# Attention on pooled keys and two feed-forward layers on one Trainium2 core: four changes of place, VectorE for GpSimd, GpSimd for TensorE

## The chip, the cores and the metric

The kernel runs on one core of one Trainium2 chip. The metric is the device time of one execution in microseconds. A time is the median of several runs; besides, one execution was taken apart by the hardware profiler, and every row below comes from that one. Engines are called as in the profile: PE is TensorE (PEld its weight load, which overlaps with PE), DVE is VectorE, ACT is ScalarE, POOL is GpSimd, and SP is the engine whose queue issues the DMAs.

## The reference

```
B, H, S, D = 8, 8, 576, 64
k_p = k.reshape(B, H, 72, 8, D).mean(axis=3)          # keys and values: means of 8 rows
v_p = v.reshape(B, H, 72, 8, D).mean(axis=3)
attn = softmax(q @ k_p.T / 8)                          # 576 x 72 per head
x = (attn @ v_p) -> [4608 tokens, 512]
h = x @ w_in1;  g = 0 if h <= -1, h if h >= 1, else (h + 1)**2 / 4;  x2 = g @ w_out1
h = x2 @ w_in2; r = max(h, 0);  out = (r * r) @ w_out2    # w_in 512 x 2048, w_out 2048 x 512
```

All is float32. The two layers take nearly all of the work.

## The kernel before

**Split products.** A float32 product is made of three products in the type fp32r: each operand is split in a high part (a copy that ScalarE rounds to fp32r) and a low part (the difference, by VectorE), and TensorE adds high times high, high times low and low times high. For the weights the parts are `wihi`, `wilo`, `wohi`, `wolo`; for the activations `xhi`, `xlo`, `gh`, `gl`.

**Steps.** Layer one goes in 9 blocks of 512 tokens by 16 pieces of the hidden dimension, in 144 steps, and 16 more steps start layer two. In step s, `gemm1(s)` makes `ph` in 12 matmuls (L666), ScalarE and VectorE make `g` from it (L689, L690, L699) and split it (L701, L707), and `gemm2(s - 2)` adds to four PSUM banks in 12 matmuls (L738). `ph` has two buffers: `gemm1(s + 2)` waits for VectorE's `g` of step s. In the steps for which `whole` says so, `gemm2` takes `g` and the weight unsplit, in plain float32 (L727); each such matmul shows as two records in the trace.

**Attention inside the steps.** The queries come in 36 tiles of 128 tokens. A tile's attention is cut in units, and tables (`slots`, `pool_at`) put at most two into a step: scores (`pss`, L372), softmax on VectorE and ScalarE, the product with the values (`px`, L488). The attention of the first four tiles stands ahead of step 0, in the head of the program. The rest of layer one's blocks wait for the tiles that make their input, so all goes in one order.

**Pooling.** Keys and values of a batch come in 8 pieces (4 of keys, 4 of values, two heads each) into a pool of three buffers. For batch 0, VectorE adds rows for the keys and GpSimd for the values (L284), and TensorE does the rest. For batches below `ON_PE` TensorE does all the pooling, in matmuls of the raw piece with the identity (`pk`, L309, and `pv`, L329). For the others GpSimd pools each piece in three additions (L297 twice, L298), and TensorE only turns the pooled keys (L314).

**Queries.** Tiles below `TURNED` come by one or two DMAs and are turned by TensorE (`pq`, L356), which ScalarE copies out of PSUM. The others come by 16 or 32 small DMAs, already cut in blocks of 32, and VectorE turns each block (L347).

**Weights.** Every weight is mapped from the bits of its load by ScalarE, VectorE (L153, L156, L159) and one integer addition of GpSimd (L162): those of layer one in the head and steps 0 to 15, those of layer two (`z`) in 16 groups between steps 28 and 140. A group (`prepare_w2`) takes two pieces, keeps their quarters as high and low parts in DRAM (`keep_w2`, tile `cb`, L172 and L173), makes four sums of quarters (L196 to L199, for a product with 7 instead of 8 partial products) and keeps these too. The second layer then reads them back.

**Order.** Instructions are put on each engine's queue by a scheduler that works from the program's order; each engine then takes its own queue in order, and the one SP queue issues all DMAs.

Of the kernel before, what the change touches and what calls it, by code (L numbers as in the profile page):

```python
# [23 lines left out]

TURNED = 11

# [5 lines left out]
def pooled_attention_moe_moe(  # L32
# [59 lines left out]

    ON_PE = 3
    NK = -(-SP // TR)
# [73 lines left out]

    def keep_w2(kind, g, n, two, lo_on):

        c = cv.tile([P, 2, 2, HB], F32R, tag="st", name="cb")
        nc.scalar.activation(out=c[:, :, 0, :], in_=two, func=AF.Copy)  # L172
        lo_on.tensor_tensor(out=c[:, :, 1, :], in0=two, in1=c[:, :, 0, :].bitcast(F32), op=ALU.subtract)  # L173
        nc.sync.dma_start(out=w2c[kind][g][:, n:n + 2], in_=c.bitcast(F32))

    def prepare_w2(kind, g):

        two = []
        for i in range(2):
            f = g + i * NG  # L180
            stage_w(kind, 1, f)
            yield
            conv = convert_w(kind, 1, f)
            for _ in conv:
                pass
            two.append(halves(w_sb.pop((kind, 1, f))).rearrange("p (a c) -> p a c", a=2))
            yield
            keep_w2(kind, g, 2 * i, two[i], nc.vector)
            yield
# [5 lines left out]
        s1, s2, s3, s4 = s12[:, 0, :], s12[:, 1, :], s34[:, 0, :], s34[:, 1, :]  # L195
        nc.gpsimd.tensor_tensor(out=s1, in0=a21, in1=a22, op=ALU.add)  # L196
        nc.gpsimd.tensor_tensor(out=s2, in0=s1, in1=a11, op=ALU.subtract)
        nc.gpsimd.tensor_tensor(out=s3, in0=a11, in1=a21, op=ALU.subtract)
        nc.gpsimd.tensor_tensor(out=s4, in0=a12, in1=s2, op=ALU.subtract)  # L199
        yield  # L200
        keep_w2(kind, g, 4, s12, nc.gpsimd)
        yield
        keep_w2(kind, g, 6, s34, nc.gpsimd)
        yield
# [74 lines left out]
    def pool_kv(nm, b, p):  # L279
        if b == 0:  # L280

            a = kv_t[nm, b, p]
            for w in (4 * D, 2 * D):
                (nc.vector if nm == "k" else nc.gpsimd).tensor_tensor(  # L284
                    out=a[:, :, 0:w], in0=a[:, :, 0:w], in1=a[:, :, w:2 * w], op=ALU.add
                )
        if b < ON_PE:
# [227 lines left out]
    for t in range(TB0, NTILE):  # L515
# [10 lines left out]
        if t in first_tile:  # L526
            b = first_tile.index(t)
            todo.update({2 * c - 2 + i // 2: ("k", b, i) for i in (0, 2)})
            if b < ON_PE:
                todo.update({at_v: ("v", b, i) for at_v, i in zip(((7, 9), (37, 39))[b - 1], (0, 2))})  # L530
            for i in range(2 * NP if b >= ON_PE else 0):
# [94 lines left out]
    def whole(kind, s):  # L626

        return kind == "o" and s < KF

# [524 lines left out]
```

## Time and profile before

| | |
|---|---|
| median of 3 runs | 1673.24 us (1672.28, 1673.24, 1678.28) |
| the profiled execution's own time | 1679.75 us |
| its span | 1677.7 us |
| mean granted clock of TensorE | 0.989 of full speed |
| busy: PE, DVE, ACT, POOL | 98%, 74%, 53%, 20% of the span |

The span runs from the first to the last instruction; the execution's time holds 2.05 us more. The clock of 1.00 is 2.4 GHz, and 0.50 is 1.2 GHz; shares between them are means over a stretch. The busy shares are means over stages: the head (0 to 43 us), steps 0 to 15 with the weights of layer one (43 to 215 us), layer one with the preparation of layer two's weights (up to 884 us, where GpSimd's last instruction ends), then the rest of layer one and layer two.

### The profile page before, as it was taken

What the parts mean: (1) busy time and instruction counts of PE and PEld (TensorE: products, weight loads), DVE (VectorE), ACT (ScalarE), POOL (GpSimd) and SP (SyncE); (2) the same over time, 40 slices, a digit from 0 to 9 for tenths busy, and PEclk for the clock granted to TensorE, in tenths of its full rate; (3) what the DMA queues carried; (4) which work ended last, traced back from release to release, by engine and by line L of the source; (5) the groups of instructions that cost most, each with busy time, mean ns of one, the idle gap of its engine ahead of it and who ended that gap; (6) DMA issues with size and microseconds to landing.
All of it is one profiled execution on the core that took longest, in us unless ns stands there. A gap on an engine that the chain in (4) does not pass through costs nothing.

```text
span 1677.7 us, 23589 instructions
## 1 busy us (share of the span) xinstructions
PE 1640.4 (98%) x7952; PEld 1322.4 (79%) x7952; DVE 1237.9 (74%) x1973; ACT 885.0 (53%) x1603; POOL 327.6 (20%) x299
## 2 busy tenths in 40 slices
PE   7899999999999899999999999999999999999998
PEld 6665788888887687878888888888888878887886
DVE  5998578888888888888886452569557856885585
ACT  5655455656566465766666542346435533553353
POOL 3444144542435515231230000000000000000000
PEclk7999999999999999999999999999999999999999
DMA  9475535435354445443543085567686777677675
GB/s 240 134 217 152 144 83 155 148 108 161 112 158 141 118 122 181 123 132 103 192 170 128 7 295 176 170 193 231 191 255 218 207 204 238 213 207 227 194 206 135
DMA packets 276728, 284.72 MB, mean 170 GB/s; under 512 B 151168, under 2 KB 179840, under 8 KB 276608
## 3 DMA queue, kind: packets, MB, share of 16 engines
q1 hardware_dynamic: 276608, 283.21, 56.4%
q8 instruction: 64, 1.05, 0.3%
q14 instruction: 56, 0.46, 0.1%
HBM read 218.10 MB, written 65.01 MB: 169 GB/s over the span
## 4 chain that ended last, share of the span: by engine, by line
PE 84%; DVE 8%; DMA 3%; issue 2%; ACT 1%; POOL 1%; SPq 1%; DVEq 0%; POOLq 0%; ACTq 0%
PE ph L666 22%; PE acc L738 20%; PE dp L1012 10%; PE cp L1003 10%; PE dq L1012 5%; PE cr L1003 5%; PE cq L1003 3%; PE dr L1012 3%; PE px L488 2%; PE pss L372 2%; PE acc L727 2%; DVE wilo L221 1%; DMA w<-w2i 1%; DVE wolo L221 1%; DMA st<-in_moe_w_out_dram 1%
## 5 line engine op out<-in xcount | busy, mean ns | idle before, releaser
L666 PE MATMUL ph<-xhi,wihi 128*128 128x512 f32 x576 | 233.4, 406 | 6.8 <-DVE g L699 5.7
L666 PE MATMUL ph<-xlo,wihi 128*128 128x512 f32 x576 | 226.4, 393 | 0.0
L666 PE MATMUL ph<-xhi,wilo 128*128 128x512 f32 x576 | 226.2, 393 | 0.0
L960 ACT ACTIVATE gh<-g 128x512 fp32r<-128x512 f32 x224 | 139.7, 630 | 151.7 <-DVE g L1029 48.0
L738 PE MATMUL acc<-gh,wohi 128*128 128x512 f32 x512 | 205.9, 402 | 0.0
L738 PE MATMUL acc<-gh,wolo 128*128 128x512 f32 x512 | 200.1, 391 | 1.5 <-DVE wolo L221 1.5
L738 PE MATMUL acc<-gl,wohi 128*128 128x512 f32 x512 | 200.2, 391 | 0.0
L1003 PE MATMUL cp<-x,w 128*128 128x512 f32 x768 | 187.0, 390 | 1.0 <-DMA w<-w2i 0.7
L768 DVE TENSOR_TENSOR gl<-g,gh 128x512 fp32r<-128x512 f32 x224 | 151.3, 687 | 47.6 <-ACT gh L960 46.2
L1003 PEld LDWEIGHTS cp<-x,w 128*128 128x128 f32 x768 | 143.5, 188 | 33.6 <-issue 2.2
L221 DVE TENSOR_TENSOR wilo<-wi,wihi 128x512 fp32r<-128x512 f32 x144 | 123.4, 857 | 58.3 <-ACT wihi L217 57.3
L1012 PE MATMUL dp<-gh,w 128*128 128x512 f32 x512 | 161.5, 389 | 0.0
L707 DVE TENSOR_TENSOR gl<-g,gh 128x512 fp32r<-128x512 f32 x144 | 114.3, 794 | 56.7 <-ACT gh L701 54.1
L666 PEld LDWEIGHTS ph<-xhi,wihi 128*128 128x128 f32 x576 | 109.2, 190 | 35.2 <-DVE g L699 6.1
L217 ACT ACTIVATE wihi<-wi 128x512 fp32r<-128x512 f32 x144 | 89.8, 624 | 81.2 <-PE ph L666 81.0
L666 PEld LDWEIGHTS ph<-xhi,wilo 128*128 128x128 f32 x576 | 109.3, 190 | 23.5
L666 PEld LDWEIGHTS ph<-xlo,wihi 128*128 128x128 f32 x576 | 109.3, 190 | 22.4 <-issue 1.0
L701 ACT ACTIVATE gh<-g 128x512 fp32r<-128x512 f32 x128 | 80.3, 628 | 84.1 <-DVE g L699 83.5
L297 POOL TENSOR_TENSOR kv<-kv 72x512 f32<-72x512 f32 x80 | 93.7, 1173 | 158.4 <-DMA kv<-in_k_dram 81.6
L221 DVE TENSOR_TENSOR wolo<-wo,wohi 128x512 fp32r<-128x512 f32 x128 | 109.2, 853 | 15.3 <-ACT wohi L217 15.1
L1025 ACT ACTIVATE s<-cp 128x512 f32<-128x512 f32 x96 | 57.2, 595 | 118.7 <-PE cp L1003 118.7
L738 PEld LDWEIGHTS acc<-gh,wolo 128*128 128x128 f32 x512 | 96.3, 188 | 21.4 <-DVE wolo L221 2.9
(144 smaller groups left out, 3208.7 us busy)
## 6 DMA issues: line engine op xcount, KB each, us to landing
w<-w2i SPq DMA_DIRECT2D x224, 256.0 KB
w<-w2o SPq DMA_DIRECT2D x224, 256.0 KB
w2i<-cb SPq DMA_DIRECT2D x32, 512.0 KB
w2o<-cb SPq DMA_DIRECT2D x32, 512.0 KB
st<-in_moe_w_out_dram SPq DMA_DIRECT2D x31, 512.0 KB
st<-in_moe_w_in_dram SPq DMA_DIRECT2D x29, 512.0 KB
pd<-pad SPq DMA_DIRECT2D x32, 384.0 KB
z<-pd SPq DMA_DIRECT2D x96, 128.0 KB
```

The source lines that it names most:

```text
L217: nc.scalar.activation(out=hi, in_=src, func=AF.Copy)
L221: eng.tensor_tensor(out=lo, in0=src, in1=hi.bitcast(F32), op=ALU.subtract)
L297: nc.gpsimd.tensor_tensor(out=a[:, :, 0:w], in0=a[:, :, 0:w], in1=a[:, :, w:2 * w], op=ALU.add)
L666: nc.tensor.matmul(out=ph, lhsT=a[:, kk % a.shape[1], :], rhs=c[:, kk, :], start=(i == 0), stop=(i == 3 * KD - 1))
L701: act(out=gh, in_=g, func=AF.Copy)
L707: nc.vector.tensor_tensor(out=gl, in0=g, in1=gh.bitcast(F32), op=ALU.subtract)
L738: nc.tensor.matmul(out=o, lhsT=lhsT, rhs=rhs, start=(f == 0 and x == 0), stop=(f == KF - 1 and x == 2),)
L768: tt(out=out, in0=a, in1=b, op=ALU.subtract)
L960: act(out=hi, in_=a, func=AF.Copy)
L1003: nc.tensor.matmul(out=out[0], lhsT=w[:, a, k, :], rhs=xq[b, i][c][:, k, :], start=(n == 0 and i in (1, 2, 7)), stop=(n == 5), skip_group_ ...
L1012: nc.tensor.matmul(out=out[d], lhsT=w[:, a, d, :], rhs=x[c], start=(g == 0 and n == 0 and i in (1, 2, 7, 4)), stop=(g == NG - 1 and n == 2 ...
L1025: act(out=snaps[key], in_=a, func=AF.Copy)
```

## The change

Four things change. (1) The low parts and the sums in `prepare_w2` that GpSimd made are made by VectorE. (2) `ON_PE` goes from 3 to 2, so batch 2 is pooled by GpSimd, at places that `pool_at` gives, instead of by TensorE in matmuls; VectorE also adds the rows of batch 0's values. (3) `WHOLE` is 10: steps 0 to 9 instead of 0 to 15 take `gemm2` in unsplit float32, and steps 10 to 15 are split. (4) `TURNED` goes from 11 to 8.

```diff
+WHOLE = 10
-TURNED = 11
+TURNED = 8
...
-    ON_PE = 3
+    ON_PE = 2
...
-    def keep_w2(kind, g, n, two, lo_on):
+    def keep_w2(kind, g, n, two):
...
-        lo_on.tensor_tensor(out=c[:, :, 1, :], in0=two, in1=c[:, :, 0, :].bitcast(F32), op=ALU.subtract)
+        nc.vector.tensor_tensor(out=c[:, :, 1, :], in0=two, in1=c[:, :, 0, :].bitcast(F32), op=ALU.subtract)
...
-        nc.gpsimd.tensor_tensor(out=s1, in0=a21, in1=a22, op=ALU.add)
-        nc.gpsimd.tensor_tensor(out=s2, in0=s1, in1=a11, op=ALU.subtract)
-        nc.gpsimd.tensor_tensor(out=s3, in0=a11, in1=a21, op=ALU.subtract)
-        nc.gpsimd.tensor_tensor(out=s4, in0=a12, in1=s2, op=ALU.subtract)
+        nc.vector.tensor_tensor(out=s1, in0=a21, in1=a22, op=ALU.add)
+        nc.vector.tensor_tensor(out=s2, in0=s1, in1=a11, op=ALU.subtract)
+        nc.vector.tensor_tensor(out=s3, in0=a11, in1=a21, op=ALU.subtract)
+        nc.vector.tensor_tensor(out=s4, in0=a12, in1=s2, op=ALU.subtract)
         yield
-        keep_w2(kind, g, 4, s12, nc.gpsimd)
+        keep_w2(kind, g, 4, s12)
         yield
-        keep_w2(kind, g, 6, s34, nc.gpsimd)
+        keep_w2(kind, g, 6, s34)
...
             for w in (4 * D, 2 * D):
-                (nc.vector if nm == "k" else nc.gpsimd).tensor_tensor(
-                    out=a[:, :, 0:w], in0=a[:, :, 0:w], in1=a[:, :, w:2 * w], op=ALU.add
-                )
+                nc.vector.tensor_tensor(out=a[:, :, 0:w], in0=a[:, :, 0:w], in1=a[:, :, w:2 * w], op=ALU.add)
...
-                todo.update({at_v: ("v", b, i) for at_v, i in zip(((7, 9), (37, 39))[b - 1], (0, 2))})
+                todo.update({at_v: ("v", b, i) for at_v, i in zip((7, 9), (0, 2))})
...
-        return kind == "o" and s < KF
+        return kind == "o" and s < WHOLE
```

Lines up to 283 stand two further down in the changed kernel (L162 is L164 there, L221 is L223); from L297 on they are the same.

TensorE's queue at the place where batch 2's keys are pooled (step 15), before. `acc` are the banks of `gemm2`, `wo` a weight, `gw` an unsplit activation:

```order
L666 MATMUL ph<-xhi,wilo 128x512
L309 MATMUL pk<-ident,kv 64x72 x32
L727 MATMUL acc_685<-gw,wo_1345 128x512
L727 MATMUL acc_686<-gw,wo_1345 128x512
L727 MATMUL acc_687<-gw,wo_1345 128x512
L727 MATMUL acc_688<-gw,wo_1345 128x512
L309 MATMUL pk<-ident,kv 64x72 x32
L666 MATMUL ph<-xhi,wihi 128x512
```

The same place in the changed kernel:

```order
L738 MATMUL acc_688<-gh,wolo 128x512
L488 MATMUL px<-aT,vp 64x128 x8
L314 MATMUL pk<-ident,kp 128x72 x2
L738 MATMUL acc_688<-gl,wohi 128x512
L738 MATMUL acc_685<-gh,wohi 128x512
L738 MATMUL acc_685<-gh,wolo 128x512
L666 MATMUL ph<-xhi,wihi 128x512
L314 MATMUL pk<-ident,kp 128x72 x2
```

The 64 matmuls of the raw keys are gone for 4 turns of pooled keys, and the step's `gemm2` is split.

GpSimd's queue in the changed kernel around steps 8 to 12, where it stands between the additions that finish the weights of layer one (`wo`, `wi`, L164):

```order
L164 TENSOR_TENSOR wi_1146<-low_1148,wi_1146 128x512
L164 TENSOR_TENSOR wo_1238<-low_1240,wo_1238 128x512
L164 TENSOR_TENSOR wi_1242<-low_1244,wi_1242 128x512
L297 TENSOR_TENSOR kv<-kv 72x2x256
L297 TENSOR_TENSOR kv<-kv 72x2x128
L298 TENSOR_TENSOR kp<-kv 72x128
L164 TENSOR_TENSOR wo_1312<-low_1314,wo_1312 128x512
L297 TENSOR_TENSOR kv<-kv 72x2x256
L297 TENSOR_TENSOR kv<-kv 72x2x128
L298 TENSOR_TENSOR kp<-kv 72x128
```

Before, the same additions stand there with nothing between them:

```order
L162 TENSOR_TENSOR wi_1140<-low_1142,wi_1140 128x512
L162 TENSOR_TENSOR wo_1211<-low_1213,wo_1211 128x512
L162 TENSOR_TENSOR wi_1215<-low_1217,wi_1215 128x512
L162 TENSOR_TENSOR wo_1275<-low_1277,wo_1275 128x512
L162 TENSOR_TENSOR wi_1279<-low_1281,wi_1279 128x512
```

Two of batch 2's four pieces of keys are seen here; the first stands eight additions of weights further up, the fourth two further down.

VectorE's queue in the changed kernel at the first group of layer two's weights (`s` holds two sums of quarters, `cb` the parts that are kept):

```order
L707 TENSOR_TENSOR gl<-g,gh 128x512
L198 TENSOR_TENSOR s_2770<-z 128x256
L175 TENSOR_TENSOR cb<-z,cb 128x2x256
L199 TENSOR_TENSOR s_2770<-s_2770,z 128x256
L223 TENSOR_TENSOR wilo<-wi_402,wihi 128x512
L200 TENSOR_TENSOR z<-z 128x256
L201 TENSOR_TENSOR z<-z,s_2770 128x256
L699 SCALAR_TENSOR_TENSOR g<-ph,u 128x512
L175 TENSOR_TENSOR cb<-s_2770,cb 128x2x256
L175 TENSOR_TENSOR cb<-z,cb 128x2x256
L707 TENSOR_TENSOR gl<-g,gh 128x512
```

Before, the sums and the last two low parts of this group stand on GpSimd's queue:

```order
L196 TENSOR_TENSOR s_2712<-z 128x256
L197 TENSOR_TENSOR s_2712<-s_2712,z 128x256
L198 TENSOR_TENSOR z<-z 128x256
L199 TENSOR_TENSOR z<-z,s_2712 128x256
L173 TENSOR_TENSOR cb<-s_2712,cb 128x2x256
L173 TENSOR_TENSOR cb<-z,cb 128x2x256
```

Now `wilo`, `g` and `gl` of the steps stand behind these six on VectorE.

## Rows read from the trace of the kernel before

**Rows 1.** The page: span, and busy time of each engine.

```profile
span 1677.7 us, 23589 instructions
PE 1640.4 (98%) x7952; PEld 1322.4 (79%) x7952; DVE 1237.9 (74%) x1973; ACT 885.0 (53%) x1603; POOL 327.6 (20%) x299
```

**Rows 2.** Windows of 20 us: PE, PEld, DVE, ACT, POOL busy, PEclk, DMA share, GB/s.

```profile
60.00:80.00 20.00, 16.23 (x108) 10.90 (x107) 19.35 (x35) 15.11 (x30) 8.43 (x6) 1.00 0.79 225
...
120.00:140.00 20.00, 16.64 (x77) 10.48 (x77) 19.93 (x37) 12.44 (x23) 7.62 (x6) 1.00 0.56 156
...
160.00:180.00 20.00, 20.00 (x197) 13.76 (x196) 8.67 (x13) 7.67 (x16) 7.82 (x7) 1.00 0.48 131
```

**Rows 3.** Waits of PE: us in total, times, longest.

```profile
PE pk L309 <- DVE kv L284: 7.4, 3, 5.7
PE ph L666 <- DVE g L699: 5.7, 1, 5.7
...
PE pss L372 <- DVE xlo L501: 2.3, 2, 1.7
```

**Rows 4.** Timeline of PE: start, length, instructions; a whole, then a split `gemm2`.

```profile
161.21 3.60 PE L727 MATMUL acc<-gw,wo 128*128 128x512 f32 x8
164.74 1.09 PE L488 MATMUL px<-aT,vp 72*64 72x128 f32 x16
...
203.55 0.39 PE L738 MATMUL acc<-gh,wohi 128*128 128x512 f32 x1
...
206.27 3.66 PE L329 MATMUL pv<-kv,ident 72*72 72x128 f32 x32
```

**Rows 5.** Groups of PE's instructions by form, 160 to 215 us.

```profile
L329 PE MATMUL pv<-kv,ident 72*72 72x128 f32 x64 | 7.3, 272 | 0.0
...
L309 PE MATMUL pk<-ident,kv 72*64 72x72 f32 x128 | 4.4, 228 | 0.0
...
L356 PE MATMUL pq<-ident,q 128*128 128x128 f32 x8 | 1.2, 272 | 0.0
```

**Rows 6.** The chain that ended last, 500 to 600 us: start, length.

```profile
501.04 2.82 PE ph L666 x12
...
581.67 5.49 PE ph L666 x12
```

**Rows 7.** Timeline of DVE inside the longest wait of PE.

```profile
576.52 2.42 DVE L221 TENSOR_TENSOR wilo<-wi,wihi 128x512 fp32r<-128x512 f32 x1
```

**Rows 8.** Timeline of POOL, ahead of and inside that wait.

```profile
560.59 2.55 POOL L297 TENSOR_TENSOR kv<-kv 72x512 f32<-72x512 f32 x2 [13.63 <-DMA kv<-in_v_dram]
...
572.54 4.64 POOL L297 TENSOR_TENSOR kv<-kv 72x512 f32<-72x512 f32 x4
```

**Rows 9.** Groups of POOL's instructions by form, 240 to 860 us.

```profile
L297 POOL TENSOR_TENSOR kv<-kv 72x512 f32<-72x512 f32 x33 | 47.5, 1439 | 141.5 <-DMA kv<-in_v_dram 73.7 <-DMA kv<-in_k_dram 67.8
...
L297 POOL TENSOR_TENSOR kv<-kv 72x256 f32<-72x256 f32 x33 | 29.7, 901 | 2.5
L173 POOL TENSOR_TENSOR cb<-s,cb 128x512 fp32r<-128x512 f32 x14 | 20.8, 1488 | 0.0
...
L196 POOL TENSOR_TENSOR s<-z 128x256 f32<-128x256 f32 x14 | 11.9, 852 | 1.0
...
L298 POOL TENSOR_TENSOR kp<-kv 72x128 f32<-72x128 f32 x16 | 10.1, 642 | 2.2 <-PE pk L314 1.7
```

**Rows 10.** Groups of DVE's instructions by form, 240 to 860 us.

```profile
L221 DVE TENSOR_TENSOR wilo<-wi,wihi 128x512 fp32r<-128x512 f32 x99 | 88.5, 894 | 17.7 <-ACT wihi L217 17.5
...
L173 DVE TENSOR_TENSOR cb<-z,cb 128x512 fp32r<-128x512 f32 x27 | 19.2, 711 | 13.0 <-ACT cb L172 12.9
```

**Rows 11.** Line L221 from 885 us on, where POOL is idle: ns min/median/max.

```profile
L221 DVE TENSOR_TENSOR wolo<-wo,wohi x17: 681/684/693, 884.6 to 965.0; 128x512 fp32r<-128x512 f32 x17
```

**Rows 12.** Line L284, batch 0's sums on VectorE: ns min/median/max.

```profile
L284 DVE TENSOR_TENSOR kv<-kv x8: 420/554/689, 4.4 to 10.9; 72x512 f32<-72x512 f32 x4, 72x256 f32<-72x256 f32 x4
```

**Rows 13.** Timeline of SP's queue: part of the DMAs of one turned tile.

```profile
171.34 5.85 SPq L253 DMA_DIRECT2D q<-in_q_dram  x11
```

More of the change, by code (lines that the diff above doesn't have):

```diff
@@ L187, in prepare_w2 @@
             yield
-            keep_w2(kind, g, 2 * i, two[i], nc.vector)
+            keep_w2(kind, g, 2 * i, two[i])
             yield
```

## Prediction

> **What bounds the kernel now.** The page comes first: TensorE is busy for 1640.4 of 1677.7 us, VectorE for 1237.9 [rows 1]. So only some 37 us of the span can come from waits; anything more has to come from work that TensorE no longer does. The windows then show that the share hides two different stages [rows 2]. From 60 to 140 us VectorE is full (19.35 and 19.93 of 20 us) and TensorE is not: in the two windows shown it lacks 3.8 and 3.4 us. At 160 to 180 us it is the other way round, TensorE 20.00 and VectorE 8.67. From there to the end TensorE waits almost for nothing. The list of waits says where the rest is [rows 3]: 7.4 us in the head for VectorE's sums of the first keys, which nothing here touches; short ones such as 2.3 us for `xlo`, in the full stage; and one single wait of 5.7 us for `g`.
>
> That single wait, at 576 to 582 us, is worth a look, since it is made by what the change moves. GpSimd had stood still for 13.63 us for a piece of values and then worked without a break, 4.64 us of it in four additions of pooling [rows 8], with the sums of the weight quarters among them. VectorE's `wilo` took 2.42 us in it [rows 7], where one with GpSimd idle takes 0.684 [rows 11]. `g` stood behind it on VectorE's queue. After the wait the granted clock was down, and the first 12 matmuls took 5.49 us instead of 2.82 [rows 6]. So this event cost 5.7 + 2.7 = 8.4 us.
>
> **The change on TensorE.** All of this lies at 145 to 215 us, where TensorE is the bound.
> - A whole `gemm2` takes 164.74 - 161.21 = 3.53 us, a split one 206.27 - 203.55 = 2.72 us [rows 4]. Six steps change from the one to the other: -4.9 us. The price is paid elsewhere: a rounding of `g` and of `wo` on ScalarE, and `gl` and `wolo` on VectorE, 2 x 0.68 us a step [rows 11]. VectorE had over 11 us free in 20 there [rows 2], so I take nothing for it; if it came late by its whole length in all six steps it would be 8 us.
> - Batch 2's keys and values took 4.4 and 7.3 us [rows 5]; the four turns of pooled keys that come instead cost what four `pq` cost, half of 1.2 us [rows 5]: -11.1 us.
> - The `pq` of three tiles go, 0.6 us each: -1.8 us.
>
> That is -17.8 us. Busy times hold the tail of each run's last matmul, which the next one overlaps, so I take **-17** (15 to 18).
>
> **The change on GpSimd and VectorE, weights.** In 240 to 860 us GpSimd's low parts take 1.49 us each and a sum 0.85 [rows 9]. With two and four in each of 16 groups, 16 x (2 x 1.49 + 4 x 0.85) = 102 us of GpSimd's work go. On VectorE a low part takes 0.71 [rows 10], and a sum, of half the width, about the 0.42 us that is the least of batch 0's sums [rows 12]: 16 x (2 x 0.71 + 4 x 0.42) = 50 us more for VectorE. Part comes back at once: `wilo` takes 0.894 us on average in that stage [rows 10] against 0.684 undisturbed [rows 11], and if all subtractions with both inputs in SBUF (some 300: `wilo`, `wolo` and `gl`) lose 0.2 us each, that is 60 us of stretching for all that GpSimd does there; with some two fifths of its work gone, about 25 us. So VectorE gets some 25 us more work net over 620 us, 4 points. TensorE needs `g` only two steps later, so this costs nothing while VectorE's queue stays less than a step late. What hides it is that reserve, and if it is used up the price is an event like the one above, 8.4 us. That one itself I take as gone, since GpSimd's sums and low parts that lay between the poolings are: **-8.4 us**. Both ends: 0, if another takes its place, and -8.4.
>
> How hard the two engines hinder each other is also in the Trainium skill, "SBUF — State Buffer", section "Who interferes with whom": an instruction of VectorE with two inputs in SBUF and one of GpSimd that reads SBUF exclude each other, and the later one waits for the other's whole length. The 2.42 us of `wilo` agree with that [rows 7]; the average of 0.894 says that most instructions do not meet one. By the rule the gain could be up to the 102 us of VectorE's time; the time of the kernel would not change by it, because VectorE is not the bound in that stage.
>
> **The change in the full stage.** Here it costs. GpSimd's pooling of batch 2's keys now lies in steps 8 to 12, about 100 to 150 us: four pieces of 1.44 + 0.90 + 0.64 us [rows 9], 12 us. If it hinders VectorE as GpSimd does at 240 to 860 us (0.2 us on each 0.68 at a third of the time busy, and half of VectorE's instructions of a kind that is hindered), 12 us of it cost VectorE 4 to 6 us; the ends are 0 and 12. VectorE's queue has no reserve there, but it has one from 150 us on, so a part shows on TensorE: **+3 us**. The new DMAs of tile 8 come in here too: eleven DMAs of a turned tile keep SP's queue for 5.85 us [rows 13], so 16 hold back the weights' loads queued behind by some 7 us once; it is in the +3, because the loads run ahead of their use. Tiles 9 and 10 load later, where the queue and VectorE have room; VectorE's turn in place of ScalarE's copy is nothing there.
>
> **The head.** VectorE makes batch 0's eight sums of values, 8 x 0.554 = 4.4 us [rows 12], between 19 and 30 us, and is no longer hindered by GpSimd's. It holds free time there and the chain waits for TensorE most of the time: **+1 us** (0 to 4).
>
> **Sum.** Against the profiled execution's own 1679.75 us: -17 - 8.4 + 3 + 1 = -21.4, **1658 us**. The median is 6.5 us below that execution. If it lacks the single wait, the change is -13 from 1673.24 (1660); if it has it, -21.4 (1652). Both lie around the 1658 that I keep. A change of half a per cent, 8.4 us, is about what a measurement of this kernel tells from none; faster by that means below 1664.9.
>
> **Rivals.**
> - *The wait comes back elsewhere.* VectorE gets more work in the weights' stage, and GpSimd still stands behind late pieces and then catches up. For it: VectorE's waits for rounded weights are there already (17.5 us for `wilo`, 12.9 for `cb`) [rows 10]. Against it: in 620 us there was one such event. It gives 1658 + 8.4 = 1666 with one. Chance 0.16.
> - *GpSimd blocks VectorE for the whole length in the full stage*, 12 us instead of 3, and TensorE shows it all, since it already waits there. For it: 19.93 us of 20 busy [rows 2]. Against it: the average of 0.894. It gives 1658 + 9 = 1667. Chance 0.1. The rule of the Trainium skill that is named above, in "SBUF — State Buffer", would do just this if every addition met an instruction of VectorE.
> - *Slower: VectorE becomes the bound of the weights' stage.* Its first sum of a group needs the second piece's `z` from GpSimd, which stands behind pooling that waits up to 13.63 us for a piece [rows 8]. Before, GpSimd itself stood there; now VectorE stands, with `wilo`, `g` and `gl` of the steps behind it. A wait of VectorE longer than its reserve of about a step is an event of 8.4 us or more. From two on the gain is gone (1658 + 2 x 8.4 = 1675); three give 1683, slower than 1673.24 by 0.6%. Against it: ScalarE's copy of the same `z` waits for it already today, ahead of the step's `u`, and with 16 groups only one event shows. Chance 0.08.
>
> **Chances and range.** The forecast holds with 0.66. Faster: it, and a small part of the two mild rivals: 0.70. Same: most of these two: 0.22. Slower: 0.08. The range: below, the gains at their upper ends with no cost (1658 - 4 - 1, and the 1652 of the median) and some of TensorE's short waits in the full stage gone too, 1648; above, the two mild rivals and a little more, 1671. The likeliest case's own range is 1651 to 1664.
>
> **What would show it.** Right: in the new profile TensorE's busy time is down by about 17 us, with 128 records of L309 and 64 of L329 fewer and step 16 some 13 us earlier than before; no wait of 5 us between 240 and 860 us; VectorE's `wilo` near 0.8 us there; VectorE still full from 60 to 150 us, with TensorE's idle time there some 3 us above the old. Wrong: waits of PE for VectorE of several us in the weights' stage (third rival), idle time of PE at 100 to 150 us up by 10 (second), or the six split steps late by `wolo` or `gl`. A head that ends more than 4 us later would also break it, above all if the clock of TensorE rose later.

## The result, and the profile after

The changed kernel takes 1657.03 us (median of 4 runs, 1655.25 to 1657.76), the kernel before 1672.76 in the same series; the ratio is 0.9901, with a 95% interval of 0.9874 to 0.9928. It is faster by 1.0%, and 1 us off the forecast. The stages and the experiments show that the forecast is right as a total only, and by luck: terms of the sum were wrong by 12 us in one direction and by 13 in the other.

The page of the changed kernel; it answers to [rows 1]:

```profile
span 1654.9 us, 23309 instructions
...
PE 1616.5 (98%) x7776; PEld 1312.1 (79%) x7776; DVE 1269.4 (77%) x2092; ACT 889.0 (54%) x1610; POOL 245.5 (15%) x219
```

TensorE's busy time is down by 23.9 us and the span by 22.8, so TensorE is idle as long as before. The windows of the full stage and of the one behind it answer to [rows 2]:

```profile
60.00:80.00 20.00, 20.00 (x123) 14.04 (x122) 19.73 (x33) 12.48 (x25) 9.39 (x7) 0.93 0.83 247
...
120.00:140.00 20.00, 20.00 (x90) 13.90 (x90) 19.93 (x37) 13.63 (x26) 10.87 (x10) 1.00 0.70 185
...
160.00:180.00 20.00, 19.82 (x115) 16.04 (x115) 15.38 (x25) 12.90 (x25) 8.48 (x9) 1.00 0.32 99
```

VectorE (third pair) is as full as before, and GpSimd (fifth) does more, but TensorE no longer lacks 3.8 and 3.4 us in the first two. The waits of TensorE over the whole span answer to [rows 3]:

```profile
PE pk L309 <- DVE kv L286: 8.7, 3, 6.3
PE ph L666 <- DVE g L699: 5.8, 4, 2.2
PE pss L372 <- ACT kbd L319: 4.1, 2, 3.6
PE px L488 <- DVE aT L478: 2.9, 5, 1.2
PE pss L372 <- DVE pn L397: 2.0, 1, 2.0
PE ph L666 <- DVE wi L158: 1.9, 1, 1.9
```

The single wait of 5.7 us for `g` is gone. In its place stand four shorter ones for `g`, two for `kbd` (the pooled keys that ScalarE copies out of PSUM) and some for `aT`; all but 1.4 us of these three lines lies between 240 and 860 us, in the weights' stage. VectorE's groups in that stretch answer to [rows 10]:

```profile
L223 DVE TENSOR_TENSOR wolo<-wo,wohi 128x512 fp32r<-128x512 f32 x100 | 81.2, 812 | 4.1 <-ACT wohi L219 3.9
L223 DVE TENSOR_TENSOR wilo<-wi,wihi 128x512 fp32r<-128x512 f32 x99 | 76.6, 774 | 9.3 <-ACT wihi L219 9.3
...
L175 DVE TENSOR_TENSOR cb<-z,cb 128x512 fp32r<-128x512 f32 x47 | 36.6, 778 | 17.0 <-ACT cb L174 16.4
...
L198 DVE TENSOR_TENSOR s<-z 128x256 f32<-128x256 f32 x16 | 9.8, 615 | 6.3 <-POOL z L164 6.3
L199 DVE TENSOR_TENSOR s<-s,z 128x256 f32<-128x256 f32 x16 | 9.2, 576 | 0.1
```

To see where the time went, both traces were cut at the first `ph` matmul (L666) of steps 0, 12, 21 and 128 (12 such matmuls make a step). Steps 21 to 128 hold the weights' stage. In the table a kernel's name is that of its experiment below; "waits" is the sum of TensorE's idle times between steps 21 and 128; all lengths in us. Medians are of different series; that of the kernel before moved between 1672.76 and 1675.04 among them, so the ratios are the better comparison.

| kernel | head | 0 to 12 | 12 to 21 | 21 to 128 (waits) | rest | median | ratio to before, 95% |
|---|---|---|---|---|---|---|---|
| before | 43.0 | 100.0 | 72.8 | 660.7 (8.6) | 801.2 | 1672.76 | 1 |
| before_again | 41.5 | 104.2 | 72.8 | 660.4 (8.8) | 800.1 | | |
| changed | 38.3 | 96.1 | 57.8 | 663.9 (11.3) | 798.9 | 1657.03 | 0.9901 [0.9874, 0.9928] |
| u_sums | 36.0 | 96.5 | 57.8 | 676.9 (19.8) | 803.4 | 1674.40 | 0.9999 [0.9983, 1.0014] |
| u_onpe | 36.3 | 97.1 | 68.5 | 650.4 (2.2) | 799.8 | 1653.26 | 0.9870 [0.9842, 0.9897] |
| u_whole | 35.7 | 99.4 | 60.5 | 655.4 (4.6) | 798.0 | 1649.67 | 0.9846 [0.9821, 0.9872] |
| u_v0 | 36.9 | 99.6 | 64.5 | 667.1 (13.5) | 801.2 | 1668.11 | 0.9960 [0.9943, 0.9977] |
| u_turned | 35.6 | 100.7 | 61.3 | 650.5 (1.4) | 798.8 | 1649.15 | 0.9858 [0.9836, 0.9881] |
| b_sums | 38.3 | 100.0 | 72.7 | 648.6 (0.4) | 800.4 | 1661.43 | 0.9931 [0.9905, 0.9957] |
| null_s | 37.6 | 96.3 | 57.8 | 666.0 (11.5) | 801.7 | 1660.22 | 0.9916 [0.9898, 0.9935] |
| kv_ahead | 36.2 | 101.6 | 62.5 | 668.3 (15.1) | 799.3 | 1667.58 | 0.9946 [0.9928, 0.9964] |
| z_dve | 36.0 | 96.2 | 57.8 | 652.2 (3.2) | 798.8 | 1643.38 | 0.9806 [0.9781, 0.9830] |
| p2 | 36.4 | 96.3 | 57.8 | 647.9 (0.0) | 799.6 | 1640.60 | 0.9787 [0.9763, 0.9811] |
| sums_z | 38.3 | 96.7 | 57.8 | 674.2 (19.3) | 799.5 | 1667.38 | 0.9954 [0.9936, 0.9971] |

The stage takes 648 us with no wait and about 1.4 us more for each us of waits ((663.9 - 647.9) / 11.3 = 1.4, (676.9 - 647.9) / 19.8 = 1.5). In the changed kernel the larger part of what goes beyond the waits is TensorE's clock. Of its nine waits in the stage only the longest, 3.6 us for `kbd` from 610 us on, has a lower granted clock behind it (the column after the five engines):

```profile
605.00:610.00 5.00, 5.00 (x24) 3.87 (x22) 4.42 (x4) 1.58 (x3) 4.77 (x5) 1.00 0.48 155
610.00:615.00 5.00, 1.44 (x6) 1.29 (x6) 4.43 (x9) 3.93 (x9) 1.22 (x2) 0.74 0.42 138
615.00:620.00 5.00, 5.00 (x15) 3.90 (x14) 4.67 (x9) 3.82 (x9) 0.00 (x0) 0.58 0.22 34
```

TensorE stood still, and in the next window the granted clock is 0.58 and only 15 matmuls fit where 24 did. What the two windows lack of full speed, 0.26 and 0.42 of 5 us, is 3.4 of the 4.7 us beyond the waits (663.9 - 647.9 - 11.3).

### The profile page after: what moved, and what is told of

The parts are those of the page before. It is cut to its first block, busy times and chain, and to the rows that moved or that the text cites. A ratio compares the mean times of both kernels' runs of the same rounds, so it can differ in the third digit from the quotient of the medians.

```text
span 1654.9 us, 23309 instructions
## 1 busy us (share of the span) xinstructions
PE 1616.5 (98%) x7776; PEld 1312.1 (79%) x7776; DVE 1269.4 (77%) x2092; ACT 889.0 (54%) x1610; POOL 245.5 (15%) x219
## 4 chain that ended last, share of the span: by engine, by line
PE 60%; DVE 6%; ACT 2%; DMA 2%; SPq 1%; issue 1%; POOL 1%; DVEq 0%; POOLq 0%; ACTq 0%
PE acc L738 12%; PE ph L666 11%; PE dp L1012 11%; PE cp L1003 10%; PE dq L1012 5%; PE cr L1003 5%; PE dr L1012 3%; PE cq L1003 3%; POOL z L164 1%; DVE pad L441 1%; DVE wolo L223 1%; DVE wilo L223 1%; SPq L255 1%; DMA st<-in_moe_w_in_dram 1%; DVE cb L175 1%
## 5 line engine op out<-in xcount | busy, mean ns | idle before, releaser
L666 PE MATMUL ph<-xhi,wihi 128*128 128x512 f32 x576 | 231.8, 402 | 7.8 <-DVE g L699 5.8
L666 PE MATMUL ph<-xlo,wihi 128*128 128x512 f32 x576 | 225.8, 392 | 0.0
L666 PE MATMUL ph<-xhi,wilo 128*128 128x512 f32 x576 | 225.4, 391 | 0.0
L960 ACT ACTIVATE gh<-g 128x512 fp32r<-128x512 f32 x224 | 139.2, 630 | 150.2 <-DVE g L1029 47.9
L738 PE MATMUL acc<-gh,wohi 128*128 128x512 f32 x536 | 216.6, 404 | 0.0
L738 PE MATMUL acc<-gl,wohi 128*128 128x512 f32 x536 | 210.4, 393 | 0.0
L738 PE MATMUL acc<-gh,wolo 128*128 128x512 f32 x536 | 210.0, 392 | 0.0
L297 POOL TENSOR_TENSOR kv<-kv 72x512 f32<-72x512 f32 x96 | 114.8, 1196 | 261.4 <-DMA kv<-in_v_dram 137.4
L223 DVE TENSOR_TENSOR wilo<-wi,wihi 128x512 fp32r<-128x512 f32 x144 | 116.1, 806 | 37.1 <-ACT wihi L219 34.5
L701 ACT ACTIVATE gh<-g 128x512 fp32r<-128x512 f32 x134 | 84.2, 629 | 110.2 <-DVE g L699 110.0
L666 PEld LDWEIGHTS ph<-xhi,wihi 128*128 128x128 f32 x576 | 108.5, 188 | 36.9 <-DVE g L699 7.5
L666 PEld LDWEIGHTS ph<-xhi,wilo 128*128 128x128 f32 x576 | 108.7, 189 | 23.2
L666 PEld LDWEIGHTS ph<-xlo,wihi 128*128 128x128 f32 x576 | 108.8, 189 | 21.7 <-issue 0.7
L738 PEld LDWEIGHTS acc<-gl,wohi 128*128 128x128 f32 x536 | 101.1, 189 | 22.4
L738 PEld LDWEIGHTS acc<-gh,wohi 128*128 128x128 f32 x536 | 101.3, 189 | 20.4 <-issue 1.2
```

Source lines behind the costliest of these rows:

```text
L223: eng.tensor_tensor(out=lo, in0=src, in1=hi.bitcast(F32), op=ALU.subtract)
L297: nc.gpsimd.tensor_tensor(out=a[:, :, 0:w], in0=a[:, :, 0:w], in1=a[:, :, w:2 * w], op=ALU.add)
L666: nc.tensor.matmul(out=ph, lhsT=a[:, kk % a.shape[1], :], rhs=c[:, kk, :], start=(i == 0), stop=(i == 3 * KD - 1))
L701: act(out=gh, in_=g, func=AF.Copy)
L738: nc.tensor.matmul(out=o, lhsT=lhsT, rhs=rhs, start=(f == 0 and x == 0), stop=(f == KF - 1 and x == 2),)
L960: act(out=hi, in_=a, func=AF.Copy)
```

## The experiments

**Each part undone alone.** Four kernels, each the changed one with one part back.

```diff
# u_sums
+        nc.gpsimd.tensor_tensor(out=s1, in0=a21, in1=a22, op=ALU.add)
...
+        keep_w2(kind, g, 4, s12, nc.gpsimd)
+        keep_w2(kind, g, 6, s34, nc.gpsimd)
# u_onpe
+    ON_PE = 3
+                todo.update({at_v: ("v", b, i) for at_v, i in zip(((7, 9), (37, 39))[b - 1], (0, 2))})
# u_whole
+WHOLE = 16
# u_v0
+                (nc.vector if nm == "k" else nc.gpsimd).tensor_tensor(
+                    out=a[:, :, 0:w], in0=a[:, :, 0:w], in1=a[:, :, w:2 * w], op=ALU.add
+                )
```

> The changed kernel with the four sums of each weight quarter and the low parts of these sums back on GpSimd. Theory of the prediction (the sums on VectorE removed one wait of 5.7 us and the 2.7 us of lower clock behind it): that wait comes back, one wait of TensorE of about 5 us for the keys between 560 and 620 us, 1665 us in all, ratio to the kernel before 0.995. Rival that the two traces suggest (between step 21 and step 128 the change lost 2.6 us, so that the sums on VectorE cost several small waits for g, keys and aT with clock losses that come to more than the one wait): 1654 us, ratio 0.9885. Third: what matters is the order in which the queues come out, not the engine that adds; then the time stays within 2 us of 1657 and the waits stand in other places.

> The changed kernel with batch 2 pooled by TensorE again, keys and values. Theory of the prediction (11.1 us of TensorE work that the change takes out): TensorE busy 10 to 11 us more, about 1668 us, ratio 0.9965, the loss made between steps 12 and 21. Rival (GpSimd's pooling of batch 2 held VectorE up between 60 and 150 us, so that its absence gives 3 us back ahead of step 12): 1665 us, ratio 0.995, with steps 9 to 12 some 3 us earlier than in the changed kernel.

> The changed kernel with the first sixteen steps of the second product in whole float32 again instead of ten. Theory of the prediction (six steps, 0.81 us each of TensorE work): TensorE busy 4.9 us more, 1662 us, ratio 0.993. Rival (VectorE is full up to 150 us and the six more low parts of the out weights, 0.6 to 0.9 us each, hold it up, so the split was partly paid for): 1658 us, ratio 0.9905, with fewer waits of TensorE before step 16.

> The changed kernel with the eight sums of batch 0's values back on GpSimd. Theory of the prediction (the head costs 1 us with them on VectorE): step 0 starts at 37 us and the whole takes 1656 us, ratio 0.9895. Rival (the head ended 4.8 us earlier because of this part, GpSimd's sums having held the head up): step 0 starts at 43 us, 1662 us, ratio 0.993, and the granted clock is 0.50 again from 26 to 45 us. Third: the head owes its 4.8 us to something else in the change (other work moved out of it, or another order): step 0 stays at 38 us and the time within 1 us of 1657.

Measured: with the sums back the whole gain is gone (1674.40). The stage grows by 13 us, and a wait of 5.7 us for `g`, as in [rows 3], is there again among others:

```profile
PE ph L666 <- DVE g L699: 12.3, 5, 5.7
PE pss L372 <- ACT kbd L319: 4.8, 2, 3.2
PE px L488 <- DVE aT L478: 1.5, 3, 1.0
```

So the prediction's theory of this part has the right sign and is too small (8.4 us); the rival, by which the sums cost time, and the third, by which the time stays at 1657, are wrong. The next two are the surprise: with 5 us and 11 us of TensorE work put back, the kernel is faster than the changed one, by 7.4 and 3.8 us (the intervals of the ratios of u_onpe and of the changed kernel overlap, so the 3.8 alone would not be clear of the noise; the stages are). The work does cost what was forecast where it stands: steps 12 to 21 take 10.7 us more in u_onpe and 2.7 more in u_whole (and steps 0 to 12 another 3.3). But the stage behind it, whose work is the same, gets 13.5 and 8.5 us shorter. Both theories of these two runs fall. u_v0 costs 11 us, where its three expectations had 1656, 1662 and 1657: all three fall. Its head starts step 0 at 36.9 us, within the 35.6 to 38.3 of the kernels with these sums on VectorE; the loss comes later, 3.5 us in steps 0 to 12 (where the granted clock is 0.59, 0.50 and 0.89 between 65 and 80 us), 6.7 in steps 12 to 21 (with one wait of 5.0 us for `aT` and a clock of 0.78 and 0.54 between 145 and 155 us) and 3.2 in the stage. Why the waits are there, no run tells.

**The queries' part undone, the kernel before once more, the first part alone, and a change of order alone.**

```diff
# u_turned (from the changed kernel)
+TURNED = 11
# b_sums (from the kernel before): part (1) of the change, nothing else
# null_s (from the changed kernel)
-        nc.vector.tensor_tensor(out=s2, in0=s1, in1=a11, op=ALU.subtract)
         nc.vector.tensor_tensor(out=s3, in0=a11, in1=a21, op=ALU.subtract)
+        nc.vector.tensor_tensor(out=s2, in0=s1, in1=a11, op=ALU.subtract)
```

> The kernel before, unchanged, taken apart once more. The times of its 23 executions beside the first experiments lie in two heaps, 1670 to 1675 us and 1677.65 to 1682.11 us, and the profiled one (1679.75) is of the upper. First theory (the granted clock of the head, 0.50 from 26 to 45 us in that profile, makes the upper heap): in an execution of some 1671 us step 0 starts at 36 to 37 us with no such stretch, and the wait of 5.7 us at 576 us is there as before. Rival (the wait at 576 us comes and goes): step 0 at 43 us again, and no wait of over 2 us between 240 and 860 us. If the execution is of the upper heap, both expect the first profile again.

> The changed kernel with TURNED at 11 again, so that TensorE turns the queries of tiles 8 to 10. Theory of the prediction (three tiles, 0.6 us of TensorE each): TensorE busy 1.8 us more, 1659 us, ratio 0.991. Rival (the stage from step 21 to step 128, which took 648 us with next to no waits and 650 to 677 in the runs so far, goes with the order in which the queues come out): any of 1643 to 1665 us, with the difference made after step 21 and not in steps 8 to 20.

> The kernel before with the first part of the change alone: sums and low parts of the weight quarters on VectorE. Theory of the prediction (it removes the wait at 576 us and the clock loss behind it): 8.4 us, 1664.7 us, ratio 0.995, no wait of over 2 us of TensorE between 240 and 860 us. Rival from the run that undid this part (13 us between steps 21 and 128): 1660 us, ratio 0.992, stage of 648 to 652 us. Third (order of the queues alone): the stage within 3 us of the 660.7 of before, with its waits in other places, ratio 0.998 to 1.001.

> The changed kernel with two lines of the weight preparation exchanged: the third sum of quarters is written ahead of the second. Every instruction, operand and engine stays; about 95 of VectorE's 2053 rows and 50 of ScalarE's 1574 stand in another place of their queue. Theory (the load of the engines decides the stage): 1657 us within 1.5, ratio 0.990, and the same waits. Rival (the order of the queues decides it): the stage from step 21 to step 128 differs from 663.9 us by 3 to 13, with TensorE's waits in other places, 1645 to 1668 us.

before_again took 1680.78 us, again of the upper heap, so it can't decide between its theories by itself; it shows the same head and the same single wait. Its windows from 25 us on:

```profile
25.00:30.00 5.00, 4.65 (x31) 3.30 (x30) 4.83 (x14) 3.07 (x6) 1.59 (x4) 0.61 1.05 332
30.00:35.00 5.00, 5.00 (x37) 3.50 (x35) 1.89 (x2) 3.45 (x7) 2.18 (x2) 0.50 0.98 246
35.00:40.00 5.00, 5.00 (x36) 4.08 (x32) 2.54 (x5) 2.94 (x6) 0.00 (x0) 0.53 0.94 307
```

The same in b_sums, whose queues are those of the kernel before up to some 230 rows of VectorE, far behind the head:

```profile
25.00:30.00 5.00, 3.48 (x31) 2.75 (x33) 4.93 (x11) 4.00 (x9) 3.06 (x4) 1.00 1.04 346
30.00:35.00 5.00, 4.94 (x55) 3.60 (x53) 4.41 (x7) 4.39 (x9) 2.38 (x2) 1.00 1.04 250
35.00:40.00 5.00, 2.68 (x20) 1.89 (x21) 5.00 (x10) 4.73 (x10) 0.21 (x1) 0.93 1.05 303
```

The same instructions in the same order ran at 0.5 of full speed (1.2 GHz) in one execution and at 0.93 to 1.00 in the other, with step 0 at 41.5 and 38.3 us. So the head of 43.0 us in the profile of before belongs to that execution, not to its code.

u_turned is 7.9 us faster than the changed kernel: steps 0 to 12 and 12 to 21 cost 4.6 and 3.5 us, and the stage comes down to 650.5. The prediction's theory (1659 us) falls; the rival has the stage right, but not that steps 8 to 20 stay as they were. b_sums, the first part alone, is 11.5 us below the kernel before in its own series (1672.88), of the 15.7 that the whole change brings. Its stage is 648.6 us, as the rival from u_sums had it and not as the theory of 8.4 us, and this is its whole list of TensorE's waits in 240 to 860 us (L666 of the changed kernel is L668 here):

```profile
PE ph L668 <- DVE g L701: 0.4, 1, 0.4
```

null_s takes the second sum from a buffer that the third has just overwritten, so that part of the computation is changed, but not its work. Its waits sum to 11.5 us against 11.3, the stage is 2 us longer, and the time, 1660.22, lies 1.7 us outside its first theory's band. Four of its waits are where the changed kernel has them (265, 333, 433 and 500 us), but the longest are not: the 3.6 us at 610 us is gone, and 3.9 us stand at 659, where the changed kernel waits 1.0. So this one reordering moved waits and left their sum; it does not show that order has no part in them. It also says that 2 to 3 us between two kernels are nothing to explain.

**Late pieces, GpSimd's work, or VectorE's load.** Three kernels, made from the changed one.

```diff
# kv_ahead
-            load_kv_to(kv_pooled[0] + (1 if kv_pooled[0] > 3 * NP else 2))
+            load_kv_to(kv_pooled[0] + 2)
# z_dve
-        nc.gpsimd.tensor_tensor(out=z.bitcast(I32), in0=low3, in1=z.bitcast(I32), op=ALU.add)
+        (nc.gpsimd if m == 0 else nc.vector).tensor_tensor(out=z.bitcast(I32), in0=low3, in1=z.bitcast(I32), op=ALU.add)
# p2
-        for w in (4 * D, 2 * D):
+        for w in (4 * D, 2 * D) if b < 3 else (2 * D,):
```

> The changed kernel with every raw piece of keys and values from batch 1's values on asked for two pieces ahead of its pooling, not one; no work is added or taken. In the changed kernel GpSimd finishes the pieces from the fifth of batch 3 on 3 to 10 steps later than in the kernel before, and TensorE waits 11.3 us between steps 21 and 128; in three kernels where it finishes them about as early as before these waits come to 0.4 to 2.2 us and the stage to 648 to 651 us. Theory (late pieces make these waits): the pieces come earlier again, the stage falls to 652 us or less, 1645 us in all, ratio 0.983. Rival (the time at which pieces come does not matter; VectorE has too much work in the stage): the stage stays within 3 us of 663.9 and the whole within 3 of 1657.

> The changed kernel with the integer addition that finishes layer two's weights on VectorE instead of GpSimd (which changes how that sum is rounded): some 32 instructions of about 0.7 us more for VectorE, 32 of 1.6 us fewer for GpSimd, and VectorE's sums no longer wait for GpSimd. Theory (GpSimd's bursts that hold VectorE up, and the wait for its addition, make the waits of the stage): 652 to 656 us for the stage, 1647 us, ratio 0.984. Rival (VectorE's load is the limit of the stage): 22 us more for VectorE make the waits longer, stage of 668 us or more, 1662 us, ratio 0.993.

> The changed kernel without the first of GpSimd's three additions of each raw piece of batches 3 to 7 (that part of the pooling is left out): 40 instructions of 1.2 to 1.4 us, about 50 us of GpSimd's work between steps 18 and 106, VectorE's work unchanged. Theory (GpSimd's work is what stretches VectorE, which makes the waits): VectorE's stretched time falls by a third, the waits of the stage from 11.3 us to 4 or less, the stage to 654 us or less, 1647 us, ratio 0.984. Rival (VectorE's own load): VectorE's instructions keep their lengths within 5%, and the stage stays at 661 us or more.

kv_ahead fails both of its theories (the stage is 668.3 us, the whole 1667.58) and settles neither, since the pieces hardly come earlier. GpSimd pools the fifth piece of batch 3 in step 24 instead of 27, and the sixth of batch 4 in step 47 instead of 50, but 17 of the 40 pieces of batches 3 to 7 come no earlier than in the changed kernel. Against the kernel before, these 40 pieces are pooled 7.7 steps later on average in the changed kernel (those from the fifth of batch 3 on 2 to 14 steps, not the 3 to 10 of the expectation) and 6.0 steps later here; in b_sums, u_turned and u_onpe it is -0.2, 0.8 and 2.8. The waits grow to 15.1 us, and by the ratios the kernel is slower than the changed one by 0.45% of the time before. Pieces that are 6 to 8 steps late are not enough for the waits, though: z_dve and p2, which come next, have them more than 7 steps late.

z_dve refutes VectorE's load as the limit: its stage is 652.2 us, as its theory had it, where the rival had 668 or more. VectorE has more to do (third pair of the window 240 to 860 us) than in any other kernel here, and TensorE (first pair) waits less than in the changed one:

```profile
240.00:860.00 620.00, 616.80 (x3128) 502.34 (x3128) 570.99 (x986) 401.60 (x742) 105.28 (x105) 1.00 0.51 157
```

The same stretch of the changed kernel:

```profile
240.00:860.00 620.00, 608.66 (x3077) 494.66 (x3076) 555.62 (x943) 393.38 (x729) 156.86 (x136) 0.99 0.49 151
```

GpSimd's busy time fell by 51.6 us, VectorE's rose by 15.4, and the kernel is 13.7 us faster. With 1643.38 us it is the fastest here that leaves nothing out, 1.9% below the kernel before, and the version to keep of these. That the addition is rounded in another way on VectorE was assumed in the expectation; no run here shows it. In p2, GpSimd's first pooling addition is left out for batches 3 to 7 and nothing is given to VectorE. All waits in the stage are gone:

```profile
240.00:860.00 620.00, 620.00 (x3147) 506.19 (x3146) 541.49 (x963) 409.67 (x752) 101.54 (x101) 1.00 0.51 158
```

VectorE runs 963 instructions there instead of 943, in 541.49 us instead of 555.62. Its `wilo` takes 734 ns instead of 774, `wolo` 766 instead of 812. So without this part of GpSimd's work the waits do not arise. The mean lengths alone do not decide, however: in u_onpe `wilo` and `wolo` are as long as in the changed kernel, and it waits 2.2 us, not 11.3:

```profile
L223 DVE TENSOR_TENSOR wolo<-wo,wohi 128x512 fp32r<-128x512 f32 x103 | 83.1, 807 | 5.5 <-ACT wohi L219 5.3
...
L223 DVE TENSOR_TENSOR wilo<-wi,wihi 128x512 fp32r<-128x512 f32 x102 | 79.7, 782 | 15.7 <-ACT wihi L219 15.6
...
L175 DVE TENSOR_TENSOR cb<-z,cb 128x512 fp32r<-128x512 f32 x47 | 33.5, 714 | 13.7 <-ACT cb L174 12.9
```

**Amount or handshake.** z_dve removes GpSimd's work and also a wait of ScalarE for it. The last run was to tell the two apart: the sums go back to GpSimd, the integer addition stays on VectorE.

> Sums and low parts of the quarters back on GpSimd, and in their place the integer addition of layer two's weights on VectorE (as in the run before that moved it alone, rounded in another way). GpSimd's work in the stage would be about 215 us, between the 171 of the changed kernel (stage 663.9) and the 266 of the run with the sums back (676.9). First theory (the amount of GpSimd's work in the stage decides, whatever it is): 668 to 671 us for the stage, 1665 us in all, ratio 0.995. Rival (the integer addition is what hurts, since ScalarE's rounding of the weights waits for it, 63 us in all and up to 6.3 us in one piece in the changed kernel, with the steps' work behind it): 652 to 658 us, 1648 us, ratio 0.984.

The stage is 674.2 us and the whole 1667.38. The rival's wait of 63 us is gone and its forecast with it; the amount theory expected 668 to 671 and is nearer, though it is short by 3 us. A handshake is left, however, which neither text reckoned with. With the sums on GpSimd, ScalarE's rounding of them waits for GpSimd:

```profile
ACT cb L174 <- POOL s L199: 19.1, 13, 5.0
...
ACT cb L174 <- POOL z L201: 14.9, 11, 1.7
```

So the run does not separate the amount from every handshake. The same move of the addition takes 11.7 us off the stage where the sums are on VectorE (663.9 to 652.2) and 2.7 where they are on GpSimd (676.9 to 674.2). With 204.77 us of GpSimd in 240 to 860 us the waits are 19.3 us, with 248.15 (u_sums) 19.8, with 156.86 (changed) 11.3, with 105.28 (z_dve) 3.2 and with 101.54 (p2) 0. Over all kernels the amount does not decide either: the kernel before has 229.97 us of GpSimd's work there and waits 8.6 us, kv_ahead has 154.46 and waits 15.1.

## Why the prediction was right, and where it was wrong

**What a wait of the stage is made of.** At 265.4 us the changed kernel waits 0.94 us for `g`. GpSimd had waited 14.16 us for a piece of values and then worked without a break; its timeline, with start and length:

```profile
253.74 2.25 POOL L297 TENSOR_TENSOR kv<-kv 72x512 f32<-72x512 f32 x2 [14.16 <-DMA kv<-in_v_dram]
...
256.88 1.29 POOL L164 TENSOR_TENSOR z<-st,z 128x512 int32<-128x512 int32 x1
258.14 2.88 POOL L297 TENSOR_TENSOR kv<-kv 72x512 f32<-72x512 f32 x2
...
261.59 2.62 POOL L297 TENSOR_TENSOR kv<-kv 72x512 f32<-72x512 f32 x2
```

VectorE in the same time:

```profile
256.52 2.21 DVE L223 TENSOR_TENSOR wolo<-wo,wohi 128x512 fp32r<-128x512 f32 x1
258.65 1.78 DVE L707 TENSOR_TENSOR gl<-g,gh 128x512 fp32r<-128x512 f32 x1
...
262.10 1.50 DVE L199 TENSOR_TENSOR s<-s,z 128x256 f32<-128x256 f32 x1
263.53 1.23 DVE L223 TENSOR_TENSOR wilo<-wi,wihi 128x512 fp32r<-128x512 f32 x1
...
265.28 0.41 DVE L201 TENSOR_TENSOR z<-z,s 128x256 f32<-128x256 f32 x1
265.61 0.68 DVE L699 SCALAR_TENSOR_TENSOR g<-ph,u 128x512 f32<-128x512 f32 x1
...
267.42 0.68 DVE L707 TENSOR_TENSOR gl<-g,gh 128x512 fp32r<-128x512 f32 x1
```

The first four take 1.23 to 2.21 us; `gl` takes 1.78 us there and 0.68 once GpSimd has stopped. `g` stands behind them. It is the event of [rows 7, 8], in small. The Trainium skill, "SBUF — State Buffer", section "Who interferes with whom", has an instruction of VectorE with two inputs in SBUF and one of GpSimd that reads SBUF exclude each other; these rows agree with it.

The longest wait of the stage, the 3.6 us for `kbd` at 610 us, has one link more. From the chain that ended last there (start, length):

```profile
605.58 1.11 DVE cb L175
606.69 0.88 DVE s L198
607.56 0.87 DVE gl L707
608.43 1.70 DVE wolo L223
610.13 0.87 DVE s L199
...
611.02 0.03 ACT cb L174
...
613.37 0.29 ACT kbd L319
```

GpSimd is busy for 4.77 of the 5 us from 605 us on. Against 0.68 us for a full and 0.41 for a half width, as in the rows above once GpSimd has stopped, VectorE's five instructions are 2.6 us longer in all, an estimate from these rows. ScalarE's rounding of the sums (`cb`) waits for the second sum, and `kbd` stands behind it on ScalarE's queue.

Now the steps of the prediction, in their order.

- **TensorE's work, -17.** Right in place and in its sum: steps 12 to 21 are 15.0 us shorter, and undoing `ON_PE`, `TURNED` and `WHOLE` gives back 10.7, 3.5 and 2.7 us there, where 11.1, 1.8 and 4.9 were reckoned. Step 16 starts 14.4 us earlier, as the 13 of the forecast asked, but by luck: 8.7 of these stem from the head and steps 0 to 12. What failed is that these terms were added to the total as if nothing behind them could take them back. Each of the three, undone alone, makes the kernel faster, since the stage behind is then 8.5 to 13.5 us shorter.
- **The single wait gone, -8.4.** The mechanism was right, and in the kernel before it is worth more: in b_sums the wait is gone and the stage 12.1 us shorter. It is worth as much beside the other three parts: with the sums on GpSimd (u_sums) the stage of the changed kernel is 13.0 us longer. Yet that stage is 3.2 us longer than before, since the other three parts together cost it 16.2 us with the sums on GpSimd (660.7 to 676.9) and 15.3 with them on VectorE (648.6 to 663.9). This is the step of the prediction that failed: what these three do to the weights' stage was put at nothing, without a reason, and the worst end of the term was "0, if another takes its place". The rival that the wait comes back elsewhere, with its 8.4 us and a chance of 0.16, is nearest to what happened in this stage, with nine short waits, 11.3 us in all, in place of one long and three short (8.6); of its two reasons, more work for VectorE is not enough, as b_sums shows (the same sums on VectorE, 0.4 us of waits), and late pieces stay open.
- **VectorE's load costs nothing while it is less than a step late.** Right: z_dve loads it more and is faster. The estimate of the stretching was right too: `gl`, `wilo` and `wolo` lose 53 us against 0.684 each in the kernel before and 31 in the changed one in 240 to 860 us; reckoned were 60, and 25 less. The sentence that less stretching would not change the kernel's time, because VectorE is not the bound, was wrong: p2 takes nothing but GpSimd's work away, and the stage is 16 us shorter. At this load it takes GpSimd's work beside it to make `g` late.
- **The full stage, +3.** Wrong in sign (and the 7 us in it for 16 DMAs of a tile would be 8.5 by [rows 13]). Steps 0 to 12 are 96.1 us instead of 100.0, and all seven profiles of kernels that leave steps 0 to 12 as the change has them, or nearly so (u_onpe among them), show 96.1 to 97.1. GpSimd's pooling of batch 2 hinders VectorE there (`wilo` takes 1.07 us on average, 0.87 in u_onpe), but undoing it (u_onpe) makes this stretch no shorter. TensorE's waits in it went down, not up by 3: 8.1 us before, 4.2 in the changed kernel. They go with `TURNED`: 7.2 to 8.3 us in the four profiles with 11 (u_turned among them, 4.6 us longer here), 3.9 to 5.7 in the ten with 8. Undoing `WHOLE` makes the stretch 3.3 us longer and the values' sums 3.5, the first by a granted clock of 0.54 and 0.78 between 80 and 90 us, the second as said above; whether the change or the execution makes these, was not tried. before_again, with 104.2 us where the first profile had 100.0 and a clock of 0.50 and 0.59 between 75 and 85 us, shows that single profiles of one kernel differ by as much.
- **The head, +1.** There is no such cost beyond what executions differ by: u_v0 has the head at 36.9 us. The 4.7 us by which the new profile's head is shorter come from the clock in that execution of the kernel before: b_sums, with the same head at 0.93 to 1.00, starts step 0 at 38.3 us as the changed kernel does.
- **The base of the sum.** The sum was made against a profiled execution of 1679.75 us, 6.5 above the median, and the text left open why. Of the 23 that stood beside the first experiments 7 lie at 1677.65 us and above; both that were profiled are that long and ran their head at half the clock. Whether every long one did, was not seen. The text had two values from the median, 1660 if that execution lacks the single wait and 1652 if it has it. b_sums, 11.5 us below the median with a stage that lacks little else than that wait, speaks for the second, which is 5 us too low; the 1658 between them was near by luck.

So the head and its clock (-5.7 against forecast) and the full stage (-6.9) hid that the weights' stage was forecast too short (+11.6). Steps 12 to 21 (+2.0) and the time behind step 128 (-2.3, forecast as 0) make up the rest.

The second rival, GpSimd blocking VectorE for its full length in the full stage, is refuted by the waits there. The third, VectorE as the bound, did not come: VectorE's first sums wait 6.3 us for `z` in the whole stage, and more load makes it no slower. But its sign, waits of TensorE for VectorE of several us in the weights' stage, did come (5.8 us for `g`), without the slower kernel that was to follow.

**What stays open.** Why the stage of the changed kernel has 11.3 us of waits, and 1.4 to 2.2 with `TURNED` or `ON_PE` undone, although the work behind step 21 is the same. GpSimd's work is needed for the waits (p2). Among the kernels that have the same work there, the waits also follow what GpSimd still has to do in 240 to 860 us: 142.75 us with 1.4 us of waits (u_turned), 148.51 with 2.2 (u_onpe), 152.55 with 4.6 (u_whole), 156.86 with 11.3 (changed). But kv_ahead does not fit (154.46 with 15.1), and 14 us of GpSimd's work for 10 us of waits is far more than u_sums gives, where 91 us more brought 8.5 us. The time at which pieces come is not excluded, as kv_ahead moved it too little.

That it is which of GpSimd's bursts meet which instructions of VectorE is only argued. The traces have a sign of it. VectorE's low parts of the quarters (`cb<-z`, L175) run beside a busy GpSimd for 30 to 33% of their time, and take 778 to 804 ns, in the four kernels with 11.3 to 15.1 us of waits and the sums on VectorE (changed, null_s, u_v0, kv_ahead). In the six with 0 to 4.6 us (b_sums, u_turned, u_onpe, u_whole, z_dve, p2) it is 5 to 19%, and 685 to 737 ns. Late pieces would bring GpSimd's pooling to where the weights are prepared; no run moved the pieces alone far enough to show it.

## What to carry to other kernels

Work taken from the bottleneck is not a gain until the stage behind it has been looked at: undo each part of a change alone, and compare the stages by the steps' start times, not only the totals. Where GpSimd's work stretches VectorE's instructions, giving work to the busier VectorE can pay: moving 32 additions brought 13.7 us here, and 7.0 where the sums were on GpSimd (u_sums to sums_z). Before a sum is made against a profiled execution, see whether it lies in the middle of the times or at their end.

## What was not expected of the hardware

- The same head ran at a granted clock of 0.50 for some 24 and 14 us in two executions of the kernel before and at 0.93 to 1.00 up to 40 us in b_sums, which is worth 3 to 5 us. Ahead of it, from 20 to 25 us, TensorE was busy for 2.69 and 2.76 of 5 us in the first two and for 3.73 in the third. The two took 1679.75 and 1680.78 us, where medians of the kernel before are 1673 to 1675.
- TensorE's waits in the stage cost 1.4 to 1.6 times their length in all kernels here with more than 4 us of them, measured from the 647.9 us of the stage without waits. In the changed kernel the lower clock, behind one of nine waits, is 3.4 of the 4.7 us beyond them; what the rest is, no row shows.
- The integer addition of a weight took GpSimd about 1.6 us, and VectorE, where the trace of z_dve shows it as a custom instruction on twice as many elements of half the size, 0.82 us:

```profile
L164 DVE CUSTOM_DVE_ANT_0 z<-st,z 128x1024 uint16<-128x1024 uint16 x31 | 25.4, 820 | 0.4
```
